# Loading and transposing the first batch in fp32 at the start of a fused attention and gated-MLP kernel

## The chip, the cores and the metric

One core of one Trainium2 chip runs the whole program. The metric is the time of one execution on the device, in microseconds (us); a lower number is better.

## The reference

For each of 8 batches and 8 heads there are 512 tokens `x` and 32 state vectors `state`, both of width 64. Two attentions read each other; their outputs are put together along the sequence (544 rows a batch), the heads side by side (512 columns), and go through a gated MLP.

```python
scores = x @ state^T / 8;   xread = softmax(scores) @ state     # 512 rows a head
scores2 = state @ x^T / 8;  sread = softmax(scores2) @ x        # 32 rows a head
t = concat([xread, sread], rows)  ->  [8 * 544, 512]
out = (relu(t @ w_gate) * (t @ w_val)) @ w_out                  # d_ff = 1536, fp32 in and out
```

Inputs are fp32; the kernel computes in bf16 with fp32 sums.

## The kernel before

The kernel never forms `xread`. Because `xread = A @ state`, the product with a weight is `A @ (state @ w)`. So for each batch it makes `U = state @ w` for the gate and the value weights (`c_unit` for batches 0 and 1 in column slices, `u_unit` later; `up`/`upc` in the profile, line L263), and multiplies the transposed attention `ANS` with it (`gv`, L290). ScalarE takes the relu of the gate half (`relu`, L314), VectorE multiplies it with the value half into `h_sb` (`mult`, L318), and TensorE multiplies `h_sb` with `wo_sb` (`out_mms`, L327).

Ahead of that, each batch needs: `x` in SBUF as bf16 (`xb`), its transpose `xT` (16 blocks of 128x128), the scores (`att_sc`, L170: `xT` against the transposed state `stT`), their exponentials (`att_exp`, L177), the sums and reciprocals (`att_sum`, L183 and L185), the scaled attention `a_sn` (`att_scale`, L189), and its transpose into `ANS` (`att_T`, `att_out`, L205 and L219). The second attention needs the tokens once more, padded with a column of ones (`x_pad`, GpSimd, L225; `sr_mm`, L233).

The order of the work on every engine is written out by hand. A string of words lists the steps of the first 50 us: a step's name, its arguments, and after `@` the PSUM banks. So `xT.0.8.4@4` transposes blocks 8 to 11 of batch 0 into bank 4, `xo.1.0.8.dve` copies blocks 0 to 7 of batch 1 from PSUM on VectorE, `sc.0.1` are the scores of the second four heads of batch 0, `ex` their exponential, `nr` their sums, `nx` the scaling, `dw.0.128.128` loads 128 columns of the gate weights from column 128, `dx` loads a batch of `x`, and `spin` are matmuls on constants whose results nobody reads. Each engine runs its own instructions in this order and waits where an operand isn't there. Loops write the order from batch 2 on.

Loads: `nc.sync` (SP) and `nc.scalar` (ScalarE) issue on hardware queues, which copy fp32 as it is. `nc.gpsimd` issues on a software queue, whose loads also convert fp32 to bf16. At the start:

- ScalarE's queue loads the state of batches 0 and 1, then pair 1 (heads 2 and 3) of batch 0; SP's loads pair 0 (heads 0 and 1). A pair is 256 KB in fp32 and lands in `xf`.
- `x_conv_pair` (L138) converts pair 0 on ScalarE and pair 1 on VectorE into `xb[0]`.
- GpSimd's queue loads heads 4 to 7 of batch 0 straight into `xb[0]`. Then GpSimd makes the identity matrix that TensorE's transposes use, loads batch 1 in two halves, and then the weights in 14 pieces, gate and value in turn (L103).

TensorE's order there is: 8 spins, the state's transposes, a spin, `xT.0.0.4` (pair 0), a spin, `xT.0.4.4` (pair 1), a spin, `sc.0.0`, two spins, `xT.0.8.4`, `xT.0.12.4` (pairs 2 and 3), a spin, `xT.1.0.8`, `sc.0.1`, a spin, `sc.1.0`, `xT.1.8.8`, and so on to `gv.0.0`. VectorE's is: `xo.0.0.4`, a copy of the transposed state (`sto.0.1`), `nr.0.0`, `xo.1.0.8`, `nx.0.0`, `nr.0.1`, `nx.0.1`, `nr.1.0`, a copy to `ANS`.

Of the kernel before, what the change touches and what calls it, by code (L numbers as in the profile page):

```python
# [8 lines left out]
FP32 = mybir.dt.float32  # L9
BF16 = mybir.dt.bfloat16  # L10
# [6 lines left out]
def kernel(  # L17
# [9 lines left out]
    nc = tc.nc  # L27

    B, H, S, D = x.shape
# [3 lines left out]
    NJ = H // 2  # L33
    NC = S // 128
# [3 lines left out]
    def pool(name, bufs, space=None):  # L38
        if space is None:
            return ctx.enter_context(tc.tile_pool(name=name, bufs=bufs))  # L40
        return ctx.enter_context(tc.tile_pool(name=name, bufs=bufs, space=space))

    const = pool("const", 1)
    upool = pool("upool", 3)
    xin = pool("xin", 1)
    att = pool("att", 2)
    small = pool("small", 4)
    anspool = pool("anspool", 3)
    hpool = pool("hpool", 3)
# [6 lines left out]
    HK = H // NK  # L56
# [3 lines left out]
    wv_sb = const.tile([128, NJ, d_ff], BF16, name="wv_sb")  # L60
    wo_sb = const.tile([128, NF, d_model], BF16, name="wo_sb")
    id128 = const.tile([128, 128], BF16, name="id128")
    NX, DP = 2, 66
    xa = const.tile([128, NX, NC * H, DP], BF16, name="xa")
    st_f = const.tile([128, B // 2, 4, D], FP32, name="st_f")
# [3 lines left out]
    stT = const.tile([128, 2, B, H, Ns], BF16, name="stT")  # L69
# [6 lines left out]
    xf, xb, xT, e_sn, a_sn, ANS, U, hsb, sr_sb = {}, {}, {}, {}, {}, {}, {}, {}, {}  # L76
    copy = {"act": nc.scalar.copy, "dve": nc.vector.tensor_copy, "pool": nc.gpsimd.tensor_copy}
# [3 lines left out]
    def bank(name, kind="r"):  # L81

        if given:
            n = given.pop(0)
        elif kind == "spare":
            n = 6 + turn["o"] % 2
        else:
            n = (4, 3, 2, 1, 0, 5)[turn["r"] % 6] if kind == "r" else 6 + turn["o"] % 2
            turn[kind] += 1
        return psum.tile([128, 512], FP32, name=name, tag=f"b{n}")  # L90

    held = {}


    def state_dma(eng, lo, hi):
        src = state.rearrange("(g b) h (m i) d -> (b h m) g i d", b=2, i=4)
        eng.dma_start(out=st_f[:, lo // 2:hi // 2], in_=src[:, lo // 2:hi // 2])

    def xb_alloc(b):
        xb[b] = att.tile([128, H, NC, D], BF16, name="xb", tag="xb", bufs=4)  # L100
# [33 lines left out]
        copy[eng](out=state_dst(g, half).rearrange("p b h n -> p (b h) n"),  # L134
                  in_=held["st", g][rows].rearrange("p (q n) -> p q n", n=Ns))

    def x_conv_pair(b, j, eng):
        copy[eng](out=xb[b][:, 2 * j:2 * j + 2], in_=xf[b][:, 2 * j:2 * j + 2])  # L138

    def x_blocks(b):  # L140
        return xb[b].rearrange("p h (k c) d -> p (h k) (c d)", c=2)

    def xT_alloc(b):
        xT[b] = att.tile([128, 2 * H, 128], BF16, name="xT", tag="xT")
# [5 lines left out]
    def x_T(b, lo, n):  # L150

        if b not in xT:
            xT_alloc(b)
        ps = held["xT", b, lo] = bank("xT_ps").bitcast(BF16)[:, 0:128 * n].rearrange("p (k t) -> p k t", t=128)
        for k in range(n):
            nc.tensor.transpose(ps[:, k], x_blocks(b)[:, lo + k], id128)  # L156

    def x_out(b, lo, n, eng):
        copy[eng](out=xT[b][:, lo:lo + n], in_=held["xT", b, lo])  # L159
# [61 lines left out]
    def x_pad(b):  # L221

        v = xa[:, b % NX].rearrange("p (c h) d -> p h c d", c=NC)[:, :, :, 0:D]
        for hs in (slice(0, HK), slice(HK, H)):
            nc.gpsimd.tensor_copy(out=v[:, hs], in_=xb[b][:, hs])  # L225

    def sr_mm(b, kind="r"):

# [142 lines left out]

    ctx.enter_context(tc.manual_schedule())
    nc.vector.memset(stT, 0.0)
    xf[0] = xin.tile([128, HK, NC, D], FP32, name="xf", tag="xf")
    for eng, j in ((nc.sync, 0), (nc.scalar, None), (nc.scalar, 1)):
        if j is None:
            state_dma(eng, 0, 2)
        else:
            src = x[0, 2 * j:2 * j + 2].rearrange("h (p c) d -> p h c d", c=NC)
            eng.dma_start(out=xf[0][:, 2 * j:2 * j + 2], in_=src)  # L380
    nc.scalar.activation(out=tiny, in_=nc.const_aps.tensor(0.0, (128, 1), FP32), func=AF.Exp)

    def w_load(w, lo, n):
        w_dma((moe_w_gate, moe_w_val)[w], (wg_sb, wv_sb)[w], lo, lo + n)

    xb_alloc(0)
    nc.gpsimd.dma_start(out=xb[0][:, HK:H], in_=x[0, HK:H].rearrange("h (p c) d -> p h c d", c=NC))
    make_identity(nc, id128)

    def x_load(b, part, parts):  # L390
        if part == 0:
            xb_alloc(b)
        hs = slice(H * part // parts, H * (part + 1) // parts)
        nc.gpsimd.dma_start(out=xb[b][:, hs], in_=x[b, hs].rearrange("h (p c) d -> p h c d", c=NC))

    warm_ps = psum.tile([128, 512], FP32, name="warm_ps", tag="b7")

    def spin(n, cols=512):
        for i in range(n):
            nc.tensor.matmul(warm_ps[:, 0:cols], warm[:, 0:128], warm[:, 0:cols], start=True, stop=True)  # L400

    steps = {"spin": spin, "stc": state_conv, "stT": state_T, "sto": state_out, "xc": x_conv_pair, "xT": x_T, "on": lambda: nc.gpsimd.memset(xa[:, :, :, D:D + 1], 1.0), "dw": w_load, "dx": x_load, "ds": lambda: state_dma(nc.gpsimd, 2, B), "do": wo_dma,
             "xo": x_out, 
             "sc": att_sc, "ex": att_exp, "nr": att_sum, "nx": att_scale, "aT2": att_T2, "ao2": att_out2, "aT": att_T, "ao": att_out,
             "c": c_unit, "co": c_out, "u": u_unit, "uo": u_out, "gv": gv, "re": relu, "mu": mult, "o": out_part,
             "of": fin_x, "xd": x_trans_dma, "ad": att_aT_dma, "xp": x_pad, "sr": sr_mm, "sn": sr_norm}
    program = """
    dx.1.0.2 dx.1.1.2 stc.0.1.dve stc.0.0.dve dw.0.0.128 dw.1.0.128 dw.0.128.128 dw.1.128.128 dw.0.256.256  # L410
    dw.1.256.256 dw.0.512.256 spin.8 stT.0@0 dw.1.512.256 dw.0.768.256 dw.1.768.256 dw.0.1024.256 dw.1.1024.256
    dw.0.1280.256 dw.1.1280.256 dx.2.0.1 ds do.0.6 xc.0.0.act spin.1.256 xT.0.0.4@1 xc.0.1.dve sto.0.0.act
    spin.1.128 xT.0.4.4@2 xo.0.0.4.dve sto.0.1.dve xo.0.4.4.act spin.1 sc.0.0@3 ex.0.0 nr.0.0 spin.1.256 spin.1.128
    xT.0.8.4@4 xT.0.12.4@5 xo.0.8.4.act xo.0.12.4.act spin.1 xT.1.0.8@6 sc.0.1@1 ex.0.1 xo.1.0.8.dve spin.1
    sc.1.0@0 xT.1.8.8@2 stc.1.1.pool stc.1.0.pool do.6.12 spin.1 c.0.0.128@34 nx.0.0 ex.1.0 nr.0.1 xo.1.8.8.act on
# [63 lines left out]
    for b in range(3, B):  # L479
        s = b - 1  # L480
        for i, jf in enumerate((4, 5) if b == 3 else (3, 4)):
            at(s, jf, att_half, b, i)
        for part, jf in enumerate((7, 10)):
            at(s, jf, u_block, b, part)
            paired.add(NF * s + jf)
        if b + 1 < B:
            at(s, 9, x_trans_dma, b + 1)
            at(s, 9, x_pad, b + 1)
        if b + 2 < B:
            at(s, 10, x_load, b + 2, 0, 1)  # L490
# [7 lines left out]
    for g in range(first, NF * (B + 1)):  # L498
        b, jf = divmod(g, NF)
# [47 lines left out]
```

## Time and profile before

| | |
|---|---|
| median of 3 runs | 221.42 us (221.39 to 221.61) |
| profiled execution: span from first to last instruction | 219.6 us |
| median less span: what lies around the instructions | 1.82 us |
| TensorE matmul busy | 214.0 us (97% of the span) |
| VectorE, ScalarE, GpSimd busy | 129.4, 122.8, 41.7 us |
| GpSimd's queue (software_dynamic) | 9.05 MB written, 30.9% of the 16 DMA engines' span |
| first gv matmul (L290) | 13.66 us |

The profiled execution has no time of its own beside its span; its span is set against the median of the runs. All times inside the span count from its start. A busy TensorE is not one at its peak, since matmuls are pipelined and their ends are modelled. The time to landing of a load runs from its issue to its completion.

### The profile page before, as it was taken

The page shows a single profiled execution, that of the slowest core. Times are in us where ns is not written, and L with a number is a line of the kernel's source. Part 1 is how long each engine was busy: PE and PEld are TensorE (multiplying, and loading weights), DVE is VectorE, ACT ScalarE, POOL GpSimd, SP SyncE. Part 2 cuts the span into 40 slices and gives each one's busy share as a digit, 9 for nine tenths or more (in the row PEclk, how much of TensorE's full clock was granted, in tenths as well). Part 3 has the DMA queues.
Part 4 walks back from the last instruction along what each step waited for, and adds up shares of the span by engine and source line. Part 5 has one row for each costly group of instructions (what it writes and reads, how often), then busy time and mean ns, then how long its engine had stood idle before and what let it go on. Part 6 is the DMA issues. An engine that isn't in the chain of part 4 may idle for free.

```text
span 219.6 us, 4861 instructions
## 1 busy us (share of the span) xinstructions
PE 214.0 (97%) x1957; PEld 105.5 (48%) x1957; DVE 129.4 (59%) x229; ACT 122.8 (56%) x235; POOL 41.7 (19%) x59
## 2 busy tenths in 40 slices
PE   8799999999999999999999999999999999999995
PEld 3454454454444444444444444444444445666544
DVE  5599978862987567665766487648675333222100
ACT  4699887746666565555566555746654544222222
POOL 7874059072143500040003000000000000000000
PEclk9999999999999999999999999999999999999999
DMA  7999999772949883655352105501411122222132
GB/s 164 166 194 198 196 235 174 115 195 81 134 90 145 161 140 96 143 98 102 86 133 79 51 19 142 119 16 48 102 49 54 48 48 49 51 49 74 70 95 99
DMA packets 42215, 23.65 MB, mean 108 GB/s; under 512 B 22640, under 2 KB 37872, under 8 KB 42192
## 3 DMA queue, kind: packets, MB, share of 16 engines
q0 software_dynamic: 16896, 9.05, 30.9%
q1 hardware_dynamic: 24400, 13.54, 23.5%
q10 hardware_dynamic: 896, 0.75, 1.3%
q8 instruction: 15, 0.25, 0.5%
q14 instruction: 8, 0.07, 0.1%
HBM read 18.35 MB, written 8.91 MB: 124 GB/s over the span
## 4 chain that ended last, share of the span: by engine, by line
PE 92%; DMA 3%; DVE 3%; issue 1%; POOL 0%; DVEq 0%; POOLq 0%
PE o_ps L327 39%; PE gv_ps L290 38%; PE gv_ps L307 5%; PE up L263 4%; DMA xb<-in_x_dram 3%; PE upc L263 1%; PE sr_ps L233 1%; PE sc_ps L170 1%; PE o_ps L356 1%; PE xT_ps L156 1%; DVE h_sb L318 1%; DVE a_sn L189 1%; DVE cs L183 1%; DVE xT L159 0%; DVE rc L185 0%
## 5 line engine op out<-in xcount | busy, mean ns | idle before, releaser
L327 PE MATMUL o_ps<-wo_sb,h_sb 128*128 128x512 bf16 x372 | 94.3, 379 | 0.0
L290 PE MATMUL gv_ps<-ans,U 128*128 128x512 bf16 x384 | 93.6, 379 | 0.0
L318 DVE TENSOR_TENSOR h_sb<-gv_ps,g_sb 128x512 bf16<-128x512 f32 x96 | 64.4, 688 | 48.5 <-ACT g_sb L314 47.4
L314 ACT ACTIVATE g_sb<-gv_ps 128x512 bf16<-128x512 f32 (+1 forms) x108 | 62.1, 582 | 44.1 <-PE gv_ps L290 31.5
L290 PEld LDWEIGHTS <-U 128*128 128x128 bf16 x384 | 36.4, 98 | 42.2 <-issue 0.8
L327 PEld LDWEIGHTS <-h_sb 128*128 128x128 bf16 x372 | 35.4, 98 | 40.7 <-issue 2.1
L335 ACT COPY o_sb<-o_ps 128x512 f32<-128x512 f32 x31 | 18.4, 594 | 18.2 <-PE o_ps L327 16.2
L225 POOL COPY xa<-xb 128x1024 bf16<-128x1024 bf16 x16 | 16.1, 1042 | 57.6 <-PE sr_ps L233 52.7
L275 ACT CAST U<-up 128x512 bf16<-128x512 f32 x38 | 19.9, 596 | 12.1 <-PE up L263 12.1
L275 DVE CAST U<-up 128x512 bf16<-128x512 f32 x34 | 21.5, 684 | 3.9 <-PE up L263 3.9
L177 ACT ACTIVATE e_sn<-sc_ps 128x512 bf16<-128x512 f32 x16 | 9.6, 597 | 8.9 <-PE sc_ps L170 8.9
L318 DVE TENSOR_TENSOR hs_sb<-gv_ps,g_sb 128x256 bf16<-128x256 f32 x12 | 5.1, 425 | 15.3 <-PE gv_ps L307 9.2
L183 DVE TENSOR_REDUCE cs<-e_sn 128x16 f32<-128x512 bf16 x16 | 10.9, 679 | 4.4 <-ACT e_sn L177 4.4
L189 DVE TENSOR_TENSOR a_sn<-e_sn,rc 128x512 bf16<-128x512 bf16 x16 | 10.9, 686 | 0.5
L263 PEld LDWEIGHTS <-stT 64*32 64x32 bf16 x560 | 6.5, 90 | 8.7 <-issue 7.5
L285 ACT CAST U<-upc 128x512 bf16<-128x512 f32 (+1 forms) x19 | 8.8, 524 | 1.9 <-PE upc L263 1.9
L170 PEld LDWEIGHTS <-xT 128*128 128x128 bf16 x128 | 5.8, 98 | 4.4 <-DVE xT L159 0.6
L263 PE MATMUL up<-wg_sb,stT 64*32 64x512 bf16 (+1 forms) x168 | 7.3, 349 | 0.2 <-DVE h_sb L318 0.2
L307 PE MATMUL gv_ps<-br,wv_sb 128*128 128x256 bf16 x48 | 7.2, 273 | 0.0
L307 PE MATMUL gv_ps<-br,wg_sb 128*128 128x256 bf16 x48 | 7.2, 273 | 0.0
L263 PE MATMUL up<-wv_sb,stT 64*32 64x512 bf16 (+1 forms) x168 | 7.2, 349 | 0.0
L170 PE MATMUL sc_ps<-stT,xT 128*128 128x64 bf16 x128 | 6.5, 193 | 0.6 <-DVE xT L159 0.3
(53 smaller groups left out, 113.4 us busy)
## 6 DMA issues: line engine op xcount, KB each, us to landing
out_dram<-o_sb SPq DMA_DIRECT2D x26, 256.0 KB, 2.4
xb<-in_x_dram POOLq DMA_DIRECT2D x6, 512.0 KB, 6.5
wo_sb<-in_moe_w_out_dram POOLq DMA_DIRECT2D x2, 768.0 KB, 11.0
out_dram<-o_sb SPq DMA_DIRECT2D x11, 128.0 KB, 2.4
wg_sb<-in_moe_w_gate_dram POOLq DMA_DIRECT2D x5, 256.0 KB, 8.7
wv_sb<-in_moe_w_val_dram POOLq DMA_DIRECT2D x5, 256.0 KB, 9.4
xb<-in_x_dram POOLq DMA_DIRECT2D x3, 256.0 KB, 6.0
st_f<-in_state_dram POOLq DMA_DIRECT2D x1, 384.0 KB, 11.5
```

The lines of the kernel that those rows point to most:

```text
L170: nc.tensor.matmul(ps[:, h % 2, 2 * k:2 * k + 2, h // 2 % 2], xT[b][:, 2 * h + k], stT[:, :, b, h], start=True, stop=True)
L183: nc.vector.reduce_sum(out=cs, in_=e_v, axis=AX.X)
L189: {"dve": nc.vector, "pool": nc.gpsimd}[eng].tensor_tensor(out=by_pair(a_sn[b], jp).rearrange("p r (j n) -> p r j n", n=Ns), in0=e_v, in1= ...
L225: nc.gpsimd.tensor_copy(out=v[:, hs], in_=xb[b][:, hs])
L263: nc.tensor.matmul(dst[parity][32 * j:32 * j + 32], stT[r:r + 64, parity, b, 2 * j + parity], wsb[r:r + 64, j, lo:lo + n], start=True, sto ...
L275: copy[eng](out=U[b][:, w, kc, lo:lo + 512], in_=held["u", b, w, lo][kc])
L290: nc.tensor.matmul(ps[w], U[b][:, w, kc, f0:f0 + 128], ANS[b][:, kc].rearrange("p c t -> p (c t)"), start=(kc == 0), stop=(kc == NK - 1))
L307: nc.tensor.matmul(ps[w][:, 0:nt], wsb[:, j, f0:f0 + 128], br[:, j].rearrange("p b n -> p (b n)"), start=(j == 0), stop=(j == NJ - 1))
L314: nc.scalar.activation(out=g_sb[:, 0:n], in_=ps[0][:, 0:n], func=AF.Relu)
L318: nc.vector.tensor_tensor(out=dst, in0=ps[1][:, 0:n], in1=held["g", b, jf][:, 0:n], op=ALU.mult)
L327: nc.tensor.matmul(held["o", b, tsub], src[:, jf, tsub * 128:(tsub + 1) * 128], wo_sb[:, jf], start=(jf == 0), stop=(jf == NF - 1))
L335: copy[eng](out=o_sb, in_=held["o", b, tsub])
```

## The change

All four pairs of batch 0 are now loaded by the hardware queues in fp32 (pair 1 by ScalarE's, pairs 0, 2 and 3 by SP's). They are no longer converted ahead of the transposes: TensorE transposes the fp32 blocks with an fp32 identity into a PSUM bank taken as fp32, and the copy out of PSUM gives bf16. `x_pad` of batch 0 reads the fp32 tile. That tile now lies in a buffer of the pool of `h_sb`; the pool `xin` is gone. GpSimd's first load is the first half of batch 1; after it come the fp32 identity, its copy in bf16, the second half of batch 1 and the weights. The rest of the order is kept.

```diff
-    xin = pool("xin", 1)
+    id32 = const.tile([128, 128], FP32, name="id32")
...
-    def x_conv_pair(b, j, eng):
-        copy[eng](out=xb[b][:, 2 * j:2 * j + 2], in_=xf[b][:, 2 * j:2 * j + 2])
     def x_blocks(b):
-        return xb[b].rearrange("p h (k c) d -> p (h k) (c d)", c=2)
+        return (xf if b in xf else xb)[b].rearrange("p h (k c) d -> p (h k) (c d)", c=2)
...
-        ps = held["xT", b, lo] = bank("xT_ps").bitcast(BF16)[:, 0:128 * n].rearrange("p (k t) -> p k t", t=128)
+        t = bank("xT_ps")
+        ps = held["xT", b, lo] = (t if b in xf else t.bitcast(BF16))[:, 0:128 * n].rearrange("p (k t) -> p k t", t=128)
         for k in range(n):
-            nc.tensor.transpose(ps[:, k], x_blocks(b)[:, lo + k], id128)
+            nc.tensor.transpose(ps[:, k], x_blocks(b)[:, lo + k], id32 if b in xf else id128)
...
-            nc.gpsimd.tensor_copy(out=v[:, hs], in_=xb[b][:, hs])
+            nc.gpsimd.tensor_copy(out=v[:, hs], in_=(xf if b in xf else xb)[b][:, hs])
...
-    xf[0] = xin.tile([128, HK, NC, D], FP32, name="xf", tag="xf")
-    for eng, j in ((nc.sync, 0), (nc.scalar, None), (nc.scalar, 1)):
-        if j is None:
-            state_dma(eng, 0, 2)
-        else:
-            src = x[0, 2 * j:2 * j + 2].rearrange("h (p c) d -> p h c d", c=NC)
-            eng.dma_start(out=xf[0][:, 2 * j:2 * j + 2], in_=src)
+    xf[0] = hpool.tile([128, H, NC, D], FP32, name="xf", tag="h_sb")
+    state_dma(nc.scalar, 0, 2)
+    for j in range(NJ):
+        src = x[0, 2 * j:2 * j + 2].rearrange("h (p c) d -> p h c d", c=NC)
+        (nc.scalar if j == 1 else nc.sync).dma_start(out=xf[0][:, 2 * j:2 * j + 2], in_=src)
...
-    xb_alloc(0)
-    nc.gpsimd.dma_start(out=xb[0][:, HK:H], in_=x[0, HK:H].rearrange("h (p c) d -> p h c d", c=NC))
-    make_identity(nc, id128)
...
+    x_load(1, 0, 2)
+    make_identity(nc, id32)
+    nc.gpsimd.tensor_copy(out=id128, in_=id32)
+    x_load(1, 1, 2)
...
-    dx.1.0.2 dx.1.1.2 stc.0.1.dve stc.0.0.dve dw.0.0.128 ...
+    stc.0.1.dve stc.0.0.dve dw.0.0.128 ...
...
-    ... do.0.6 xc.0.0.act spin.1.256 xT.0.0.4@1 xc.0.1.dve sto.0.0.act
+    ... do.0.6 spin.1.256 xT.0.0.4@1 sto.0.0.act
```

More of the change, by code (lines that the diff above doesn't have):

```diff
@@ L400, in spin @@
             nc.tensor.matmul(warm_ps[:, 0:cols], warm[:, 0:128], warm[:, 0:cols], start=True, stop=True)
-    steps = {"spin": spin, "stc": state_conv, "stT": state_T, "sto": state_out, "xc": x_conv_pair, "xT": x_T, "on": lambda: nc.gpsimd.memset(xa[:, :, :, D:D + 1], 1.0), "dw": w_load, "dx": x_load, "ds": lambda: state_dma(nc.gpsimd, 2, B), "do": wo_dma,
+    steps = {"spin": spin, "stc": state_conv, "stT": state_T, "sto": state_out, "xT": x_T, "on": lambda: nc.gpsimd.memset(xa[:, :, :, D:D + 1], 1.0), "dw": w_load, "dx": x_load, "ds": lambda: state_dma(nc.gpsimd, 2, B), "do": wo_dma,
              "xo": x_out,
@@ L409 @@
     program = """
-    dx.1.0.2 dx.1.1.2 stc.0.1.dve stc.0.0.dve dw.0.0.128 dw.1.0.128 dw.0.128.128 dw.1.128.128 dw.0.256.256
+    stc.0.1.dve stc.0.0.dve dw.0.0.128 dw.1.0.128 dw.0.128.128 dw.1.128.128 dw.0.256.256
     dw.1.256.256 dw.0.512.256 spin.8 stT.0@0 dw.1.512.256 dw.0.768.256 dw.1.768.256 dw.0.1024.256 dw.1.1024.256
-    dw.0.1280.256 dw.1.1280.256 dx.2.0.1 ds do.0.6 xc.0.0.act spin.1.256 xT.0.0.4@1 xc.0.1.dve sto.0.0.act
+    dw.0.1280.256 dw.1.1280.256 dx.2.0.1 ds do.0.6 spin.1.256 xT.0.0.4@1 sto.0.0.act
     spin.1.128 xT.0.4.4@2 xo.0.0.4.dve sto.0.1.dve xo.0.4.4.act spin.1 sc.0.0@3 ex.0.0 nr.0.0 spin.1.256 spin.1.128
```

## The prediction

> **What bounds the kernel now.** I read the page first (TensorE busy 97% of 219.6 us, full granted clock throughout), then the chain of waits cut to the first 16 us, then the timeline there. From 13.7 us on the chain is almost only TensorE's matmuls, so the end moves with the time at which that dense stretch begins. What begins it is this chain (start, us, what):
>
> ```profile
> 2.42 0.24 POOL id masks.py:199
> 2.66 5.95 DMA xb<-in_x_dram
> 8.61 0.05 issue
> 8.65 0.63 PE xT_ps L156 x8
> 9.29 0.02 issue
> 9.31 0.69 DVE xT L159
> 10.00 0.60 DVE a_sn L189
> 10.60 0.61 DVE cs L183
> ...
> 13.10 0.29 DVE ans L219
> 13.38 0.04 issue
> 13.43 0.30 PE upc L263 x15
> 13.73 1.83 PE gv_ps L290 x8
> ```
>
> The first half of batch 1, issued by GpSimd at 2.66, lands at 8.61; eight transposes, a copy on VectorE, and then VectorE works through batch 0's normalisation without a pause until the first real matmuls. The timeline (start, us, engine, instruction, idle before and its releaser) shows what stands beside it:
>
> ```profile
> 3.97 0.62 ACT L138 CAST xb<-xf 128x512 bf16<-128x512 f32 x1 [0.80 <-DMA xf<-in_x_dram]
> 4.64 0.40 PE L156 MATMUL xT_ps<-id,xb 128*128 128x128 bf16 x4
> 5.64 0.59 ACT L159 COPY xT<-xT_ps 128x512 bf16<-128x512 bf16 x1 [0.51 <-PE xT_ps L156]
> 6.01 0.56 PE L170 MATMUL sc_ps<-stT,xT 128*128 128x64 bf16 x8 [0.19 <-DVE stT L134]
> 7.28 0.62 PE L156 MATMUL xT_ps<-id,xb 128*128 128x128 bf16 x8 [0.54 <-DMA xb<-in_x_dram]
> 8.65 0.62 PE L156 MATMUL xT_ps<-id,xb 128*128 128x128 bf16 x8 [0.54 <-DMA xb<-in_x_dram]
> 12.84 0.25 PE L263 MATMUL upc<-wg_sb,stT 64*32 64x128 bf16 x8
> ```
>
> Batch 0's second half arrives at 7.28, batch 1's first at 8.65: TensorE waits twice, 0.54 us each. The weights are a second bound close behind. Issue plus time to landing by tile puts the second gate/value slice (6.34 + 6.5) at 12.84, exactly where TensorE first uses it, and the value columns from 1024 (13.15 + 10.8) at 23.95 against a use at 24.24. The DMA engines are full meanwhile (stretches of 0.5 us; the last columns are granted clock, DMA share and GB/s written):
>
> ```profile
> 3.00:3.50 0.50, 0.50 (x3) 0.15 (x2) 0.19 (x1) 0.17 (x1) 0.50 (x2) 1.00 1.10 387
> 4.50:5.00 0.50, 0.49 (x7) 0.28 (x5) 0.33 (x1) 0.50 (x2) 0.50 (x2) 1.00 1.38 173
> 16.50:17.00 0.50, 0.50 (x17) 0.21 (x3) 0.50 (x2) 0.50 (x2) 0.05 (x1) 1.00 1.46 195
> ```
>
> The first stretch is the hardware queues in fp32; the others are GpSimd's queue, which reads fp32 and writes bf16, so 173 and 195 written are 346 and 390 read.
>
> **The change, part by part.**
>
> *Conversions.* The fp32-to-bf16 conversions of pairs 0 and 1 go: 0.62 us on ScalarE (3.97) and 0.49 on VectorE (4.67). They stood ahead of the first eight transposes: batch 0's first pair lands at 3.9 and was transposed at 4.64. Now it can start at 4.4, when TensorE is through with the state's transposes and the spin. A gain of 0.24 there, which the wait for 8.61 hides today.
>
> *Loads.* 512 KB of fp32 moves from GpSimd's queue to SP's. By the 387 row that takes 512/387 = 1.3 us of the DMA engines; by the 346 row 512/346 = 1.5. So all that follows in GpSimd's queue comes 0.2 us earlier if the engines are the limit: batch 1's first half at about 8.4, the weight slice at 12.65. If they are not full while GpSimd's queue starts up (346 against 390 is 11% missing over 4.0 to 8.6, worth 0.5 us), the new hardware traffic fits partly into the holes and the shift is up to 0.2 + 0.5 = 0.7. That the load is now issued at 1.24 rather than 2.66 brings no more than this, since the DMA records of the trace have GpSimd's first packet only at 3.9, just as the hardware queues run dry. I take 0.4, between the ends. On the other side pair 1 (ScalarE's queue, landing at 4.7) now shares the engines with SP's pair 2, 256 KB at 387, so it may come up to 0.66 later; I take 5.2. Pairs 2 and 3 should be in by 6 to 7.5, against 7.28.
>
> The Trainium skill, "DMA: Bandwidth & Descriptors", section "Issuing engines are not separate DMA queues", says that loads issued from different engines interleave on the same 16 DMA engines and that spreading them saves only issue time. By that rule the shift would be the 0.2 alone. The rows above fit it so far.
>
> *GpSimd.* Its queue loses one load issue (0.75 to 0.89 us), and between the two halves of batch 1 it now makes an fp32 identity and copies it to bf16. The bf16 memset and select take 0.22 and 0.29; the copy of 128 columns, by the 398 ns for 256 (bf16 from fp32), 0.2. Allowing double for fp32 the bf16 identity is there at 2.13 + 1.2 = 3.3, and its first user is at 3.85: hidden by 0.5. The second half is issued at about 3.3 instead of 3.42 and the first weights at about 4.1 instead of 4.15; both then wait for over 5 us in the queue, so nothing. The pad copies of batch 0 (x_pad) read fp32: 1.04 us each now, up to 1.6 by the 398 ns row; that delays GpSimd from 37.7 to 38.9 at most, and the reader, sr of batch 0, runs at 44.0. The fp32 tile now sits in a buffer of h_sb that batch 2 first writes at 52.4: free long before.
>
> *Evictions.* PSUM is now fp32 for batch 0. VectorE's 128x512 copy goes from 0.42 us to about 0.68 (128x512 bf16 from f32, 682 ns); ScalarE's stay at 0.59 (596). The first delays stT's second copy (sto) by 0.26.
>
> *Transposes.* Sixteen fp32 transposes replace sixteen bf16 ones. No row shows one. The bf16 ones take 219 ns each from start to end, but eight take 0.62, so one every (620 - 219)/7 = 57 ns. Lower bound 57, if fp32 streams as bf16 does. Upper bound 98 + 219 = 317, a weight load and a matmul with no overlap at all; in the changed program these matmuls have no separate weight-load instruction to pull ahead. A fourfold stream is 229. I take 200 ns, near the middle of 57 and 317 (187) and nearer the 229, because the operands are twice as wide.
>
> **The sum.** Follow TensorE's fixed order with 200 ns each. Pair 0's four run from 4.4 to 5.2. Pair 1's four from 5.25 to 6.05, visible at 6.2 (219 - 57 ns of drain). ScalarE's copy is done at 6.8. The scores (sc 0.0), at 6.01 today, start at 6.85. Then 0.4 us of scores and 0.17 of spin: 7.4. The last eight run to 9.0, one spin brings it to 9.2, and only then come batch 1's transposes, today at 8.65. That is +0.55, and VectorE's chain behind them moves as a whole, because the copy at 9.31 stands ahead of everything in its queue. What is late next is VectorE to 13.4; the weights, at 12.65 or earlier, no longer bind. The dense stretch after it has no idle to give back. So 219.6 + 0.55 = 220.15 us of span; the median of the runs is 221.42, 1.82 above the span, and I carry that over: 222.0.
>
> Break-even: each 10 ns per transpose moves 9.2 by 0.16. Batch 1's arrival at 8.2 to 8.4 and today's 8.65 are crossed at about 165 ns. Below 140 the landing decides and TensorE's price is hidden.
>
> **Rivals.**
>
> *Cheap transposes, earlier stream (faster).* At 57 to 120 ns TensorE is ready by 8.0 and batch 1's landing decides, at 8.61 - 0.4 to - 0.7. The first matmuls then need the weight slice, also 0.4 to 0.7 earlier. Gain 0.5 on the middle: 220.9. For it: TensorE has 0.54 us waits in both places. Against it: 173 GB/s written is near the queue's steady rate, so the stream has little to give. The Trainium skill, "TensorE: Matmul & The Clock Gate", section "Terms", says that trn2's transpose mode is four times faster for FP32; by that reading fp32 streams once and this rival holds. No row of this case can show it yet.
>
> *Four passes (slower, more).* At 229 ns the same walk gives 7.65 + 1.83 + 0.22 = 9.7, +1.05: 222.5; at 317, 11.1, +2.45: 223.9. For it: no separate weight load to prefetch. It decides from 165 ns. This is the far part of my own case. The Trainium skill, "FP8 and Floating Point Precision", section "TensorE Precision Notes", gives true FP32 four passes, which would be this one.
>
> *Nothing (the price and the gain meet).* Transposes at 140 to 190 ns, or a stream that is 0.2 us earlier while the weights hold the first matmuls at 12.65: within 0.44 us of 221.4. What speaks for it: two bounds, VectorE's chain and the weights, lie within 0.5 us of one another, so relief of one is soon used up.
>
> *It doesn't do what it says.* If the hardware loads squeeze GpSimd's, so that batch 1 lands at 9 or later, the time is that of the slow case without dear transposes: 221.8. It is held within the range.
>
> **How the numbers follow.** A measurement of this kernel can tell about 0.2%, 0.44 us. Slower: 0.50, made of transposes at 190 to 220 ns (0.24, likeliest value 222.0), the dear end from 220 ns (0.20) and squeezed loads (0.06). The faster rival 0.28, the case of nothing 0.22. The case with 222.0 alone runs from 221.7 to 223.3. The range takes in most of the faster rival, 0.6 below the median, 220.8, and the dear end up to 255 ns or so, 223.2.
>
> **What would show it.** In the changed profile: the mean spacing of the fp32 transposes (a block of eight over its count), with 165 ns as the line between the signs; the start of batch 1's first transposes against 8.65, and whether their wait ends with the DMA or with TensorE's own work; the landing of batch 1's first half against 8.61 and of the value slice against 12.84; the start of scores 0.0 against 6.01; the start of the first gv matmuls against 13.66. I am wrong if the transposes come at under 140 ns, or if the stream of weights moves by 0.5 us or more.

## The result and the profile after

The changed kernel is slower: median 222.34 us (221.36 to 223.47, 15 runs) against 221.39 us of the kernel before (15 runs). The ratio is 1.0047, 95% interval 1.0031 to 1.0063, that is 1.04 us (0.7 to 1.4). The profiled execution has a span of 220.9 us against 219.6; it took 222.70 us, 0.36 above its median, so the 1.32 us that its profile shows are more than the usual loss.

The chain of waits of the changed kernel, cut to the first 16 us, answers to the chain of before (start, us, what):

```profile
1.75 7.03 DMA xf<-in_x_dram
8.78 0.04 issue
8.82 0.66 PE xT_ps L154 x4
9.48 0.21 PE warm_ps L397
9.70 0.46 PE xT_ps L154 x8
...
10.18 0.69 DVE xT L157
...
13.96 0.29 DVE ans L217
...
14.30 0.30 PE upc L261 x15
```

It no longer begins with batch 1's load on GpSimd's queue but with SP's third load, pair 3 of batch 0: issued at 1.75, landed at 8.78. Behind it stand four transposes and a spin, and only then batch 1's eight, whose own data landed at 8.96, 0.35 later than in the profile of before (8.61). From the copy on VectorE the chain is that of before, 0.87 us later (10.18 against 9.31). The timeline shows the same wait on TensorE:

```profile
4.46 0.60 PE L154 MATMUL xT_ps<-id,xf 128*128 128x128 f32 x4
6.30 0.61 PE L168 MATMUL sc_ps<-stT,xT 128*128 128x64 bf16 x8
6.92 0.60 PE L154 MATMUL xT_ps<-id,xf 128*128 128x128 f32 x4
8.82 0.66 PE L154 MATMUL xT_ps<-id,xf 128*128 128x128 f32 x4 [1.30 <-DMA xf<-in_x_dram]
9.53 0.61 PE L154 MATMUL xT_ps<-id,xb 128*128 128x128 bf16 x8
```

TensorE was through with pair 2 by 7.5 and idled 1.30 us for pair 3. The tile view gives the price of an fp32 transpose (ns min/median/max of one):

```profile
L154 PEld LDWEIGHTS xT_ps<-id,xf x16: 139/141/143, 4.4 to 9.1; 128*128 128x128 f32 x16
L154 PE MATMUL xT_ps<-id,xf x16: 272/273/330, 4.5 to 9.2; 128*128 128x128 f32 x16
```

Four starts 109 ns apart make the 0.60 (3 x 109 + 273); the prediction took 200. Each has a weight load of its own in the trace, 141 ns long. The starts are closer than that, so it overlaps the matmul before it.

There is a second loss, which no view above shows. The first gv matmul starts 0.87 later (14.53 against 13.66), every later multiplication into `h_sb` 0.87 to 0.93 later, the last matmul 0.93 later; the span ends 1.32 later. So 0.39 us are lost behind the last matmul: from its end to the end of the span takes 2.69 us before and 3.07 after. The waits of SP's queue in the last 6 us of the changed kernel (line waited for: us in total, times, longest):

```profile
SPq L539 <- DMA out_dram<-o_sb: 1.4, 2, 1.1
```

and of the kernel before:

```profile
SPq L542 <- DMA out_dram<-o_sb: 0.9, 3, 0.4
```

The last output lands 1.80 us behind the last matmul in both (1.79 and 1.80). A semaphore here is the counter that a DMA raises when it has landed. SP closes the program by waiting for the DMA semaphores two at a time, one entry after another, about 62 ns for an entry that is already met, in an order that the program fixes. Before, the last output's semaphore is in the last entry, and SP is through at 1.87. After, it is met at 1.82 with six entries still to go: 2.25. The trace has the DMAs of SP and ScalarE take eight semaphores in turn, and the change makes 74 of them out of 72, so the last output falls on another entry.

### The profile page after: what moved, and what is told of

Read it like the earlier page. It is cut to its first block, busy times and chain, and to the rows that moved or that the text cites. A ratio compares the mean times of both kernels' runs of the same rounds, so it can differ in the third digit from the quotient of the medians.

```text
span 220.9 us, 4837 instructions
## 1 busy us (share of the span) xinstructions
PE 211.6 (96%) x1928; PEld 106.3 (48%) x1957; DVE 129.5 (59%) x228; ACT 122.3 (55%) x234; POOL 41.2 (19%) x59
## 3 DMA queue, kind: packets, MB, share of 16 engines
q0 software_dynamic: 16368, 8.78, 29.7%
## 4 chain that ended last, share of the span: by engine, by line
PE 86%; DVE 5%; DMA 4%; issue 2%; SPq 0%; ACT 0%; DVEq 0%
PE o_ps L325 37%; PE gv_ps L288 34%; PE gv_ps L305 5%; PE up L261 4%; DMA xf<-in_x_dram 3%; DVE h_sb L316 2%; PE upc L261 1%; PE sr_ps L231 1%; PE o_ps L354 1%; PE sc_ps L168 1%; DVE cs L181 1%; DMA hs_sb<-sn 1%; PE xT_ps L154 1%; DVE a_sn L187 1%; DVE rc L183 0%
## 5 line engine op out<-in xcount | busy, mean ns | idle before, releaser
L325 PE MATMUL o_ps<-wo_sb,h_sb 128*128 128x512 bf16 x357 | 91.1, 379 | 2.3 <-issue 1.9
L288 PE MATMUL gv_ps<-ans,U 128*128 128x512 bf16 x372 | 91.9, 379 | 0.3
L223 POOL COPY xa<-xb 128x1024 bf16<-128x1024 bf16 x14 | 14.1, 1043 | 58.5 <-PE sr_ps L231 53.8
```

What stands on the lines that cost most here:

```text
L223: nc.gpsimd.tensor_copy(out=v[:, hs], in_=(xf if b in xf else xb)[b][:, hs])
L288: nc.tensor.matmul(ps[w], U[b][:, w, kc, f0:f0 + 128], ANS[b][:, kc].rearrange("p c t -> p (c t)"), start=(kc == 0), stop=(kc == NK - 1))
L325: nc.tensor.matmul(held["o", b, tsub], src[:, jf, tsub * 128:(tsub + 1) * 128], wo_sb[:, jf], start=(jf == 0), stop=(jf == NF - 1))
```

## The experiments

Each kernel's span is three terms: the start of the first gv matmul, a middle of 203.2 to 203.4 us in every profile, and the tail behind the last matmul. The ratio of the timed runs is against the kernel before on the same chip. One profile's first term scatters by 0.5 to 0.7 us between kernels that load alike (13.66 and 13.11 for before and e5, 14.53 and 13.81 for changed and e6), since the landings do; the verdicts rest on the ratios where the two differ.

| kernel | median us | ratio (95%) | pair 3 / batch 1's first half land | first gv | tail |
|---|---|---|---|---|---|
| before | 221.39 | | - / 8.61 | 13.66 | 2.69 |
| changed | 222.34 | 1.0047 (1.0031 to 1.0063) | 8.78 / 8.96 | 14.53 | 3.07 |
| e1 identity first | 222.04 | 1.0035 (1.0023 to 1.0047) | 7.84 / 8.79 | 13.85 | 3.07 |
| e2 half in fp32 | 221.57 | 1.0004 (0.9992 to 1.0016) | - / 8.36 | 13.45 | 2.72 |
| e3 converted | 223.54 | 1.0095 (1.0075 to 1.0115) | 8.63 / 8.95 | 15.57 | 3.07 |
| e4 pair 3 on ScalarE | 222.89 | 1.0068 (1.0051 to 1.0084) | 8.99 / 8.35 | 14.74 | 3.09 |
| e5 before, two DMAs more | 221.53 | 1.0023 (1.0007 to 1.0040) | - / 8.05 | 13.11 | 3.08 |
| e6 changed, two fewer | 221.79 | 1.0023 (1.0008 to 1.0039) | 8.06 / 8.53 | 13.81 | 2.72 |
| e7 load held back | 221.61 | 1.0016 (0.9999 to 1.0032) | 6.38 / 7.67 | 13.86 | 3.08 |
| e8 before, scaling earlier | 221.50 | 1.0016 (1.0002 to 1.0031) | - / 8.99 | 14.04 | 2.71 |
| e9 both causes away | 221.37 | 0.9999 (0.9985 to 1.0013) | 6.34 / 8.07 | 13.50 | 2.72 |
| e10 and fewer spins | 221.17 | 0.9993 (0.9981 to 1.0006) | 6.56 / 7.75 | 13.45 | 2.70 |

**e1_late_gpsimd.** GpSimd's first load comes behind the identity.

```diff
-    x_load(1, 0, 2)
     make_identity(nc, id32)
     nc.gpsimd.tensor_copy(out=id128, in_=id32)
+    x_load(1, 0, 2)
     x_load(1, 1, 2)
```

> Three theories of the loss of 0.95 us. Arrival: pair 3 of batch 0 lands at 8.78 because the hardware queues share the DMA engines with GpSimd's first load; TensorE and VectorE's chain then start 0.87 later. Price: the sixteen fp32 transposes, one per 109 ns and not 57, cost 16 x 52 ns = 0.83 us. Queue order: SP's third load is late because it is third in its queue, whatever GpSimd does. Here GpSimd issues its first load only after the identity (about 2.8 in place of 1.24). Arrival: pair 3 lands at 6 to 7.2, batch 1's first half at 8.5 to 9.2, the first gv matmul comes at 13.5 to 14.1 and the time is 221.2 to 221.9. Price: no change from the changed kernel, 222.3. Queue order: pair 3 still at 8.5 or later, 222.3.

The load went out at 1.59, not at 2.8, because the identity could start at 0.73. With these 0.35 us pair 3 landed at 7.84 instead of 8.78, while batch 1's first half landed no later (8.79 against 8.96). SP's loads were not touched, so this speaks against queue order; but pair 3 lands at 8.06 in e6, whose loads are those of the changed kernel, so 7.84 alone decides little. The first gv matmul came at 13.85 and the tail stayed at 3.07. The ratio, 1.0035, overlaps the changed kernel's 1.0047: a gain in time is not shown by this run.

**e2_half_fp32.** The loads of before; pairs 0 and 1 transposed as fp32 without conversion.

```diff
+        f = b == 0 and lo < 8
+        src = xf[0].rearrange("p h (k c) d -> p (h k) (c d)", c=2) if f else x_blocks(b)
...
+    nc.scalar.copy(out=id32, in_=id128)
-    ... xc.0.0.act spin.1.256 xT.0.0.4@1 xc.0.1.dve sto.0.0.act
+    ... spin.1.256 xT.0.0.4@1 sto.0.0.act
```

> The kernel before with its loads as they are, but pairs 0 and 1 transposed as fp32 with no conversion; heads 4 to 7 stay on GpSimd's queue in bf16. Arrival: batch 1's first half still lands at 8.6 and decides, so the time is that of before, 221.2 to 221.5, although eight transposes are dearer. Price: half of the 0.83 is lost, 221.8.

No difference from before: 1.0004, and the 0.4 us of the price theory (0.0019) lie outside the interval. The eight dearer transposes, and the conversions that they save, are hidden by the wait for batch 1, whose transposes start at 8.40, 0.04 behind their data.

**e3_bf16_conv.** The changed loads, with conversions and bf16 transposes.

```diff
+    def x_conv_pair(b, j, eng):
+        copy[eng](out=xb[b][:, 2 * j:2 * j + 2], in_=xf[b][:, 2 * j:2 * j + 2])
...
-    ... sc.0.0@3 ex.0.0 nr.0.0 spin.1.256 ...
+    ... sc.0.0@3 ex.0.0 nr.0.0 xc.0.2.act xc.0.3.dve spin.1.256 ...
```

> The changed kernel's loads, but all four pairs converted to bf16 (ScalarE and VectorE in turn) and transposed as bf16. Price: the loss goes, 221.4 to 221.7, however the loads land. Arrival and queue order: pair 3 lands at 8.8 as in the changed kernel, its conversion adds 0.5 and its cheaper transposes give back 0.2, so the first gv matmul is at 14.7 to 14.9 and the time 222.5 to 222.8.

The price theory falls: with bf16 transposes the time is the worst of all, 223.54. It is also 0.7 worse than the arrival theory said. In its profile the trace's clock record shows half clock from 9.8 to 13.2, and batch 1's transposes take 0.94 us there instead of 0.61. The six runs separate this part: four, the profiled one among them, have a mean granted clock of 0.990 to 0.992 and took 223.42 to 224.02; the two at 1.000 took 222.81 and 222.83. So about 1 us of the median belongs to the half-clock stretch, and without it the time is at the upper end of what the arrival theory said.

**e4_pair3_act.** Pair 3 on ScalarE's queue, behind pair 1.

```diff
-        (nc.scalar if j == 1 else nc.sync).dma_start(...)
+        (nc.scalar if j % 2 else nc.sync).dma_start(...)
```

> The changed kernel with pair 3 on ScalarE's queue, so that each hardware queue carries two pairs. Queue order: pair 3 is now second on its queue behind pair 1 and lands at 6.5 to 7.2, near pair 2; the first gv matmul comes up to 0.6 earlier, 221.7. Arrival: the same bytes share the same engines, so the later of pairs 2 and 3 lands at 8.2 or later and the time stays within 0.3 of 222.3. Price: 222.3.

```profile
9.03 0.66 PE L154 MATMUL xT_ps<-id,xf 128*128 128x128 f32 x4 [1.55 <-DMA xf<-in_x_dram]
```

Pair 3 lands at 8.99 on the other queue as well. The order within SP's queue is not the cause. The time was expected within 0.3 us of the changed kernel's and is 0.5 above it, with overlapping intervals (1.0068 against 1.0047).

**e5_before_shift.** The kernel before; two more output blocks, at about 170 us, written in halves.

```diff
-        n = 2 if 4 * B - 9 <= 4 * b + tsub < 4 * B - 4 else 1
+        n = 2 if 4 * B - 11 <= 4 * b + tsub < 4 * B - 4 else 1
```

> The kernel before with two more output blocks written as two halves each, 170 us into the run: two more hardware DMAs and nothing else. The profiles show a second part of the loss: from the last matmul to the end takes 2.69 us before and 3.07 after. At the end SP waits for the DMA semaphores in a fixed order, 62 ns a wait; the hardware DMAs take eight semaphores in rotation, so two more of them shift which wait the last output meets. Closing theory: the end comes 0.38 later, 221.7 to 221.8, with the first gv matmul unmoved. Without it: 221.4.

```profile
SPq L542 <- DMA out_dram<-o_sb: 1.4, 2, 1.1
```

The tail is 3.08 and SP's closing wait reads as in the changed kernel, although nothing at the start was touched. The ratio, 1.0023, is 0.5 us with 0.39 inside its interval. The profiled run had an early start by chance (first gv at 13.11), which is why its span hides this.

**e6_after_unshift.** The changed kernel with two output blocks written whole (`4 * B - 9` becomes `4 * B - 7`).

> The changed kernel with two output blocks written whole instead of in halves: two hardware DMAs fewer, so the same count as before. Closing theory: from the last matmul to the end 2.69 again, 0.38 less than the changed kernel, 221.9 to 222.0; the first gv matmul stays at 14.5. Without it: 222.3.

The tail is 2.72, and the ratio falls from 1.0047 to 1.0023, with intervals that overlap (1.0031 to 1.0063, 1.0008 to 1.0039). The first gv matmul was expected at 14.5 and came at 13.81 in this profile: pair 3 landed at 8.06 this time. Its arrival scatters by 0.7 between kernels that load alike (8.06, 8.63, 8.78), and with it the 0.87 of the changed kernel's profile: here it would be 0.15.

**e7_gpsimd_2p8.** As e1 with a fill on GpSimd ahead of its first load.

```diff
+    nc.gpsimd.memset(spare[:, 0:1024], 0.0)
     x_load(1, 0, 2)
```

> As the run that builds the identity first, with one more fill on GpSimd ahead of its first load, which is so issued at about 2.2 to 2.8 instead of 1.59. Arrival: GpSimd's first packets come when the hardware queues are through, pair 3 lands at 6 to 7 and batch 1's first half no later than 8.8 (the engines are full either way); the first gv matmul stays at 13.8 or comes up to 0.2 earlier, 221.9. If GpSimd's own start decides when batch 1 lands, it lands 0.6 to 1.2 later than 8.79 and the time is 222.6 or more.

Issued at 2.48, batch 1's first half lands at 7.67, earlier than in any other run, and pair 3 at 6.38. Issued at 1.24, GpSimd's load leaves pair 3 at 8.06 to 8.99 (four profiles); at 1.59, at 7.84 (one); at 2.48, at 6.34 to 6.56 (this run, e9 and e10). Stretches of 0.5 us show why; first the changed kernel, then this one (last columns: granted clock, DMA share, GB/s written):

```profile
5.00:5.50 0.50, 0.33 (x4) 0.21 (x3) 0.40 (x1) 0.13 (x1) 0.50 (x2) 1.00 1.44 183
6.00:6.50 0.50, 0.36 (x5) 0.15 (x3) 0.25 (x1) 0.50 (x1) 0.50 (x2) 1.00 1.10 232
7.00:7.50 0.50, 0.50 (x6) 0.28 (x4) 0.00 (x0) 0.50 (x1) 0.50 (x2) 1.00 1.13 141
```

```profile
4.50:5.00 0.50, 0.50 (x6) 0.50 (x5) 0.00 (x0) 0.20 (x1) 0.50 (x2) 1.00 1.07 371
5.00:5.50 0.50, 0.50 (x4) 0.50 (x4) 0.00 (x0) 0.38 (x1) 0.50 (x1) 1.00 1.15 338
6.00:6.50 0.50, 0.50 (x4) 0.50 (x3) 0.50 (x1) 0.00 (x0) 0.50 (x2) 1.00 1.43 193
```

In the changed kernel the packets of both queues lie mixed from 4.5 to 8.5. By the trace's DMA records GpSimd's first packet goes at 4.68, and from 5.0 to 5.5 its queue writes 81 KB where SP's writes 10. The last 29 KB of pair 3 then come in small lots between 7.0 and 8.42, beside 59 to 88 KB of GpSimd's in each half microsecond. Held back, GpSimd's queue has its first packet at 5.29 and leaves the engines to SP's until that is nearly through (371 and 338 up to 5.5, SP's last packet at 5.96); then it follows at 193 written, 386 read. That the mixture as such is slower is not shown. Counting GpSimd's bytes as read (twice what it writes), the engines moved 333 GB/s from 4.5 to 8.5 in the changed kernel and 363 here, but 324 in the kernel before, where GpSimd's queue has them to itself.

The first gv matmul did not follow, though: 13.86. This run met TensorE at half clock:

```profile
4.77 1.06 PE L154 MATMUL xT_ps<-id,xf 128*128 128x128 f32 x4
5.73 1.06 PE L154 MATMUL xT_ps<-id,xf 128*128 128x128 f32 x4
7.08 0.69 PE L168 MATMUL sc_ps<-stT,xT 128*128 128x64 bf16 x8
7.77 1.04 PE L154 MATMUL xT_ps<-id,xf 128*128 128x128 f32 x8
8.86 0.61 PE L154 MATMUL xT_ps<-id,xb 128*128 128x128 bf16 x8
```

The first eight fp32 transposes are 213 ns apart, the last eight 109: the trace's clock record begins full clock at 6.75 here and at 3.76 in the changed kernel's profile. (The granted-clock column of the stretches above reads 1.00 ahead of that record too; the durations tell it.) With 213 ns the scores start at 7.08 instead of 6.30, and batch 1's transposes wait for TensorE's own order until 8.86, 1.2 us behind their data. So in this profile TensorE's own order, with transposes at 213 ns, is the limit, as the prediction had it.

**e8_before_nx.** The kernel before, `nx.0.0` ahead of `xo.1.0.8` on VectorE.

> The kernel before with one instruction moved on VectorE: the scaling of batch 0's first half (0.68 us) goes ahead of the copy of batch 1's transposes, into the 1.09 us in which VectorE idles for that copy. If VectorE's chain sets the first gv matmul, the sums behind it start when their exponentials end, 0.38 earlier, and the weight slice that lands at 12.84 then holds the first gv at about 13.45: 221.15. If the copy of batch 1 itself or the weights set it already: no change, 221.4.

No gain: 1.0016. Batch 1 landed late in this profile (8.99), but against its own transposes (9.03) the first gv matmul comes 5.01 us later, exactly as before. The sums did start earlier, 1.52 behind the transposes instead of 1.87. What ends last is another chain:

```profile
11.38 1.01 ACT L159 COPY xT<-xT_ps 128x1024 bf16<-128x1024 bf16 x1
...
12.44 0.29 PEld L170 LDWEIGHTS <-xT 128*128 128x128 bf16 x8 [0.37 <-ACT xT L159]
...
12.68 0.50 PE L205 MATMUL aT_ps<-id,a_sn 128*128 128x128 bf16 x6
```

TensorE meets the scores `sc.1.1` ahead of the attention's transposes and waits there for ScalarE's copy. ScalarE's chain is as long as VectorE's. The weights stand close behind: the value slice landed at 13.23 here, 0.06 ahead of the matmuls that use it (13.29), and at 12.87 in the kernel before, 0.04 ahead of them.

**e9_both.** e7 and e6 together.

> The changed kernel with both causes taken away: GpSimd's first load held back to 2.48 by the identity and one fill, and two output blocks written whole, so that the closing waits fall as before. If closing (0.38) and arrival (0.66 of the 1.04) are the whole loss, the time is that of before within 0.4: 221.0 to 221.4; from the last matmul to the end 2.7, pair 3 landing at 6 to 7, batch 1's first half by 8. If the fp32 transposes cost on their own, 0.4 or more is left, 221.6 or above, more so in a run in which the clock rises late (213 ns a transpose at half clock, 109 at full).

0.9999: the whole loss is gone with the two causes, within 0.3 us by the interval, although the transposes are still fp32 and the clock rose late in its profile too (5.58).

**e10_both_fewer_spins.** e9 without three spins.

```diff
-    ... nr.0.0 spin.1.256 spin.1.128
+    ... nr.0.0
-    ... xo.0.12.4.act spin.1 xT.1.0.8@6
+    ... xo.0.12.4.act xT.1.0.8@6
```

> The same with the three spins left out that stand between the first scores and batch 1's transposes (0.17 and 0.22 us on TensorE). If TensorE's own order now sets batch 1's transposes, as in the profile of the run with the held-back load (they start at 8.86 though their data landed at 7.67), the first gv matmul comes up to 0.4 earlier and the time is 0.2 to 0.4 under the run with the spins. If the clock needs them, it falls for a window of 3.4 us, as it did once in the converted run from 9.8 to 13.2, and the time is 0.5 or more above it.

221.17 against 221.37, with overlapping intervals: the direction in which TensorE's own order is the limit, but not shown. The clock did not fall in its profile. No version here is clearly faster than the kernel before.

## Why the prediction was right or wrong

The forecast was 222.0, slower, with 0.50 on slower; measured 222.34. The number was near by luck: the sum put +0.55 on dear transposes, and the loss came from a late load and from the closing waits. Three of its terms failed, and by the prediction's own sign, transposes under 140 ns, it was wrong.

- *Transposes.* "I take 200 ns": mis-sized, 109 at full clock. By the prediction's own line (under 140 the price is hidden) that was the condition of the faster rival. The fourfold stream (229) and the 317 are out at full clock. 213 ns does occur, at half clock; the prediction took the clock as full throughout, from a page whose slices are 5.5 us wide. The Trainium skill, "TensorE: Matmul & The Clock Gate", section "Terms", says that trn2's transpose mode is four times faster for FP32. The trace bears this out in part: 109 ns against 57 for bf16 is 1.9 times, neither once nor four times. What they still cost in the changed kernel is pair 3's four, by an estimate 4 x 52 ns = 0.21 us of the 0.87 in its profile; e9, where pair 3 is early, shows no remainder beyond 0.3 us.
- *The walk's arithmetic.* "Each 10 ns per transpose moves 9.2 by 0.16" counts all sixteen. Pair 1's landing at 5.25 hides pair 0's four below 212 ns (4.4 + 4 x 0.212), so twelve count, 0.12 per 10 ns, and 8.65 is crossed at about 154 ns, not 165. By the same walk 255 ns gives 222.8, not 223.2. Neither changes the account, with 109 measured.
- *Loads.* "Pairs 2 and 3 should be in by 6 to 7.5": pair 3 came at 8.78, and at 8.06 to 8.99 in the four profiles that issue GpSimd's load at 1.24. In the four with the loads of before, heads 4 to 7 were in by 6.73 to 7.66. "I take 0.4" earlier for GpSimd's stream: in the changed kernel's profile it came later, 8.96 against 8.61 for the first half of batch 1 and 13.14 against 12.87 for the value slice. Over the same two sets the first half landed at 8.35 to 8.96 and at 8.05 to 8.99, so neither a gain nor a loss of this stream is shown. "The DMA engines are full meanwhile" rested on one row of the start-up, 173 written; the row from 5.5 to 6.0, below this list, has 123, and the mean from 4.5 to 8.5 is 162. The Trainium skill, "DMA: Bandwidth & Descriptors", section "Issuing engines are not separate DMA queues", says that loads issued from different engines interleave on the same 16 DMA engines and that spreading them saves only issue time. The trace agrees on the interleaving (both queues' packets from 4.5 to 8.5); the 0.2 us that the prediction took from the rule is not seen. The rival of squeezed loads, held at 0.06 and 221.8, came true in kind; it looked at GpSimd's loads (batch 1 at 9 or later, measured 8.96), while it was the hardware queue's last pair that came latest. Of the 0.87 in the changed kernel's profile, 0.35 is batch 1's own landing, and 0.52 the wait for pair 3, its transposes and a spin.
- *What carries the delay.* "VectorE's chain behind them moves as a whole" held in numbers, 0.87 on both ends. That VectorE alone sets it did not: e8.
- *The closing.* "The dense stretch after it has no idle to give back. So 219.6 + 0.55": the tail was carried over as if fixed. That the stretch itself has no idle to give held (203.25 and 203.31 us). Two more hardware DMAs cost 0.39 in the tail, over a third of the 1.04. Counting DMAs was done for the queues' issue time, not for the semaphores.
- *Right as argued:* the bf16 identity (ready at 3.06, needed at 4.12), VectorE's copy at 0.69, the pad copies (1.04 us from fp32 too), the buffer of `h_sb`, and pair 1 at 5.25 for 5.2.

The row of the kernel before against which "full" does not hold (last columns as above):

```profile
5.50:6.00 0.50, 0.32 (x3) 0.10 (x1) 0.43 (x1) 0.35 (x1) 0.50 (x2) 1.00 1.05 123
```

By the ratios, e7 takes 0.0031 and e6 takes 0.0024 off the 0.0047; together (e9) they take all of it. Each ratio is good to about 0.0016, so the split between the two causes is rough. The start is worth about 0.65 us by the timed runs (1.04 less 0.39) or 0.5 (e6, 1.0023), less than the 0.87 of the one profile.

## What to carry to other kernels

A load moved from one queue to another is not free bandwidth: where both queues are busy, ask which transfer is needed first and let the other start later; holding a load back by 1.24 us brought both in earlier here. Count the DMAs that a change adds, and look at the last two microseconds of the span as well as at the stage that was edited. One row of half a microsecond does not stand for a stage. And when one profile's stage scatters by tenths between runs, split the span into its terms before explaining a difference.

## What the runs showed of the hardware that was not expected

- Holding GpSimd's load back by 1.24 us moves its first packet by 0.6 to 0.9 us and SP's third load by about 2: with that packet at 4.51 to 4.68 us pair 3 landed at 8.06 to 8.99 (four profiles), with it at 5.29 to 5.37 at 6.34 to 6.56 (three). Batch 1's first half, on the queue held back, came earlier too: 7.67 to 8.07 against 8.35 to 8.96. Why it gains as well is open.
- TensorE's clock rose to full speed between 3.4 and 6.75 us after the span's start, differently in each of the twelve profiles, all of which begin with the same eight spins; 109 or 213 ns per fp32 transpose is the consequence. The half-clock stretch in e3's profile lasted 3.41 us, and in the other eleven profiles the clock stays full for 215.04 or 218.45 us, 63 or 64 times as long. The Trainium skill, "TensorE: Matmul & The Clock Gate", section "What's actually happening", gives a window of 3413 ns that runs freely of the kernel's start. The trace agrees: the multiples, and a spread of the rise of 3.3 us, less than one window.
- The order of the closing semaphore waits against the rotation of DMA semaphores is worth 0.39 us between kernels with 72 and with 74 DMAs on the hardware queues.
- An fp32 pad copy on GpSimd costs what the bf16 one does (1.04 us for 1024 elements).
